# An SSD, MoE and routed-MoE kernel: weights loaded in halves, eight zero products taken out, another written order

## The chip, the cores and the metric

The kernel runs on one core of one Trainium2 chip. The metric is the time of one execution on the device in microseconds (us), of which the trace shows the span from the first to the last instruction. TensorE (matrix products) is PE in the rows and its weight loads are PEld, VectorE is DVE, ScalarE is ACT, GpSimd is POOL. SyncE is SP and issues most of the DMA transfers.

## What is computed

Three stages follow each other: a chunked state-space attention (4 batches, 8 heads, 768 positions), an MoE layer that is one dense block over 3072 tokens, and a routed layer with 8 experts of which each token uses one. Shapes are in the comments.

```python
# attention, per 32-chunk: x (4,8,768,32), a (4,8,768), B and C (4,8,768,16)
cum = np.cumsum(la, axis=-1)                       # la = log(clip(a))
L = np.exp(cum[:, :, :, None] - cum[:, :, None, :]) * causal
y_intra = einsum('bhij,bhjd->bhid', einsum('bhin,bhjn->bhij', Cc, Bc) * L, xc)
y_inter = einsum('bhin,bhnd->bhid', Cc, state) * np.exp(cum)[:, :, :, None]
y[:, :, sl] = y_intra + y_inter                    # and the state is carried on
# dense layer: w_in (256,2048) and w_out (2048,256), float64
h = x @ w_in
x = np.maximum(0.01 * h, h) @ w_out
# routed layer: E=8 experts, w1 (8,256,1024), w2 (8,1024,256)
logits = x @ w_gate + modality_bias[modality_id]
e = argmax(logits); gate = softmax(logits)[e]
out = gate * (np.maximum(x @ w1[e], 0.0) @ w2[e])
```

## The kernel before

**Tiles.** The attention works in chunks of 128 positions, 24 in all (6 a batch). Four chunks make a block of 512 tokens, and the dense layer runs over blocks: for each of 16 slices f of the hidden layer, `h_mm` makes h with six products of 512 columns (two halves of w_in, each as high part times high, high times low, low times high), and `mm2` adds y with six more. The routed layer runs tiles of 512 gathered tokens of one expert with the same three-part products (`e_m1`, `e_m2`), and scatters its rows to the output with indirect DMAs from POOL (`e_sc`).

**Between h and y** stand four steps: `sa` on ACT scales h, `gg` on DVE takes the maximum, `gh` on ACT rounds it to the high part, `gl` on DVE takes what is left. h has two buffers.

**Weights of the dense layer.** w_in and w_out are float64 and are read as 64-bit integers into a tile `raw` (three buffers), a megabyte a piece: four pieces of w_in (`raw.i.k`), four of w_out (`raw.o.k`). Each piece is converted in two parts of 128x512 (`hb`, `lb` on ACT, `or` as two instructions on DVE, `cast` on ACT, and `subv` on DVE or `subg` on POOL for the low part). `part_win(k, kk)` is half kk of piece k, `part_wout(k, q)` the same for w_out. ACT's `cast` writes wih or woh, the last subtraction wil or wol.

**The start.** `decay_a` takes the logarithm of a, transposes it and makes the running sum `cum` with a product of a triangle. For chunks 0 to 3 the exponents come from products into PSUM (`bc`, `exp`). Chunk 0 needs only the logarithms. Chunks 1 to 3 need `cumb`, three bfloat16 parts of the sum: `rows` transposes cum on PE, `high` copies the first part on ACT, `out` writes the rows out (`cumrow`), `cr` on DVE takes the rest, `lows` on ACT casts it, `lowv` on DVE (L387, tile `cumb`) subtracts the third part. After `lowv` come `bc.1`, `exp.1` and so on. Later chunks load their exponents from DRAM (`cumd`, `e`).

**A chunk.** `trmm`, `trc` (tile `cm`), `trb` (tile `btt`), `trd` transpose C and B; `cb` makes their products, `mul` (tile `e`, three instructions) applies the exponents, `p3` makes the output and the state's step, `xa` on ACT and `xb` on DVE write the high and low part (`xh`, `xl`) of the block's input, `st` (tiles `pm`, `st`) carries the state. The first product of the dense layer, h.0 (L694), needs xa.3 and xb.3, the last chunk of block 0.

**Order.** Nothing is reordered by a scheduler: the string `PLAN` lists the steps, `name.chunk.part`, and each engine gets its instructions in this order. SP's DMA issues stand in it too; each has one of eight completion semaphores and waits for the DMA that had it before. Zero products (`zer`) run on PE at some places: six at the very start, two and three in `decay_a` (L346, L347 and L355), five in `warm.1.5` (L1165), four in `wy.4.1` (L1171).

Of the kernel before, what the change touches and what calls it, by code (L numbers as in the profile page):

```python
# [31 lines left out]
    trmm.3 mul.2.1 lx.3 p3.1 mul.2.0 trb.3 hb.o.0.1 trc.3 load.5 mul.2.2 bc.3.0 xa.1 lb.o.0.0 st.1 trd.3 trde.3 xb.1
    or.o.0.0 exp.3.1 p3.2 exp.3.0 bs.3 cb.3 cast.o.0.0 cd.4 st.2 trmm.4 xa.2 mul.3.1 subg.o.0.0 wy.4.1 lb.o.0.1
    mul.3.0 trc.4 le.5 xb.2 trb.4 mask.4 mul.3.2 load.6 trd.4 trde.4 hb.i.1.0 p3.3 or.o.0.1 exp.4.0 xa.3 cd.5 trmm.5
    exp.4.1 xb.3 le.6 st.3 h.0 lx.4 lb.i.1.0 trc.5 raw.o.1 bs.4 mask.5 trb.5 cast.o.0.1 load.7 trd.5 h.1 sa.0 or.i.1.0
    trde.5 exp.5.0 cb.4 subv.o.0.1 sa.1 cast.i.1.0 gg.0 mask.6 hb.i.1.1 mul.4.2 h.2 lb.i.1.1 mul.4.0 subg.i.1.0
    mul.4.1 gh.0 gg.1 trmm.6 exp.5.1 p3.4 or.i.1.1 le.7 h.3 lx.5 xa.4 gl.0 gh.1 lx.6 sa.2 st.4 y.0 trb.6 cast.i.1.1
    trc.6 xb.4 hb.o.1.0 gl.1 sa.3 cb.5 bs.5 load.8 subv.i.1.1 exp.6.0 y.1 gg.2 mask.7 mul.5.0 gh.2 mul.5.1 load.9 h.4
    mul.5.2 lb.o.1.0 gl.2 exp.6.1 gg.3 p3.5 raw.i.2 or.o.1.0 gh.3 le.8 y.2 xa.5 le.9 sa.4 bs.6 lx.7 exp.7.0 cd.7 xb.5
    h.5 load.10 gl.3 gg.4 cb.6 sa.5 cast.o.1.0 y.3 mul.6.0 hb.o.1.1 gg.5 subg.o.1.0 gh.4 mul.6.1 trmm.7 mul.6.2  # L40
    lb.o.1.1 h.6 gh.5 gl.4 trb.7 or.o.1.1 exp.7.1 p3.6 sa.6 trc.7 h.7 bs.7 le.10 xa.6 gg.6 cast.o.1.1 raw.o.2 st.6
    xb.6 raw.i.3 trd.7 y.4 trde.7 gl.5 hb.i.2.0 subv.o.1.1 cb.7 gh.6 mask.9 hb.i.2.1 y.5 mul.7.2 sa.7 mul.7.0 lb.i.2.1
    mul.7.1 trmm.8 gl.6 lb.i.2.0 p3.7 gg.7 y.6 xa.7 gh.7 xb.7 exp.9.1 or.i.2.1 h.16 exp.9.0 gl.7 h.17 or.i.2.0 sa.16
    y.7 gg.16 sa.17 raw.o.3 cast.i.2.0 bs.9 load.11 gg.17 cast.i.2.1 subg.i.2.0 h.18 pV.0 trb.8 gh.16 gh.17 gl.16 h.19
    pA.0 gl.17 hb.o.2.0 trc.8 sa.18 y.16 cd.8 lb.o.2.0 gg.18 lx.8 subv.i.2.1 trd.8 gh.18 y.17 le.11 sa.19 lx.9 gl.18
    gg.19 h.20 or.o.2.0 y.18 sa.20 gh.19 cast.o.2.0 gl.19 h.21 hb.o.2.1 gg.20 subg.o.2.0 y.19 sa.21 mask.8 gh.20 gg.21
    lb.o.2.1 h.22 gl.20 gh.21 or.o.2.1 hb.i.3.0 y.20 lb.i.3.0 sa.22 gl.21 exp.8.0 h.23 or.i.3.0 gg.22 mask.11 y.21
    sa.23 cast.o.2.1 gg.23 gh.22 h.8 cast.i.3.0 gl.22 gh.23 subv.o.2.1 h.9 sa.8 subg.i.3.0 hb.i.3.1 gg.8 lb.i.3.1 y.22
    cd.9 gl.23 sa.9 or.i.3.1 h.10 gh.8 exp.8.1 gg.9 y.23 gl.8 sa.10 cast.i.3.1 h.11 pA.1 pV.1 gh.9 subv.i.3.1 gg.10
    y.8 hb.o.3.1 bs.8 st.7 h.12 gl.9 gh.10 trde.8 sa.11 gl.10 hb.o.3.0 y.9 kg2 gg.11 sa.12 lb.o.3.0 gg.12 mask.10 h.13  # L50
    gh.11 or.o.3.0 y.10 sa.13 gl.11 cast.o.3.0 h.14 kg3 gg.13 exp.10.0 kv2 y.11 gh.12 subg.o.3.0 sa.14 lb.o.3.1 cb.8
    gh.13 gl.12 kd h.15 mul.8.0 gg.14 gl.13 y.12 sa.15 exp.11.1 gg.15 lx.10 h.24 or.o.3.1 gh.14 lx.11 y.13 mul.8.2
    cast.o.3.1 mul.8.1 sa.24 subv.o.3.1 h.25 gh.15 gl.14 cd.10 gg.24 p3.8 sa.25 load.12 gl.15 gg.25 y.14 le.12 y.15
    lx.12 gh.24 gl.24 h.26 evA.0 gh.25 evV.0 bt sa.26 lg.0 exp.10.1 h.27 lt.0 gl.25 trmm.9 sa.27 bs.10 l2.0 load.13
    trc.9 y.24 r1.0 trb.9 xa.8 r2.0 trd.9 trde.9 st.8 exp.11.0 rp.0 yr.0.0 xb.8 y.25 be.0 yc.0.0 gg.26 cb.9 gh.26 h.28
    mul.9.1 mul.9.0 mul.9.2 trmm.10 cd.11 p3.9 trc.10 gg.27 trb.10 rx.0 trd.10 le.13 st.9 trde.10 gh.27 load.14 yr.0.1
    mask.12 xa.9 h.29 yc.0.1 xb.9 sa.28 gl.26 cb.10 gl.27 y.26 mul.10.0 mul.10.1 mul.10.2 trmm.11 gg.28 p3.10 trb.11
    trc.11 gh.28 bs.11 trd.11 load.15 xa.10 h.30 cd.13 exp.12.0 xb.10 st.10 lx.13 y.27 sa.29 gl.28 trde.11 le.14 sa.30
    gg.29 lx.14 cb.11 gh.29 exp.12.1 h.31 mul.11.1 gl.29 mul.11.0 y.28 mul.11.2 cd.14 gg.30 trmm.12 p3.11 y.29 mask.13
    le.15 xa.11 trb.12 gh.30 xb.11 trc.12 sa.31 h.32 gg.31 bs.12 gh.31 gl.30 cb.12 load.16 sa.32 h.33 exp.13.1  # L60
# [1228 lines left out]
```

## Time and profile before

| | |
|---|---|
| time, median of 3 runs | 509.98 us (508.88 to 510.38) |
| time of the profiled execution | 507.78 us |
| its span, first to last instruction | 506.0 us |
| mean granted clock of TensorE | 0.996 |
| busy: PE, DVE, ACT, POOL | 491.9, 324.3, 284.9, 130.4 us |
| HBM read and written | 41.14 and 6.60 MB |

The profiled execution is 2.2 us below the median, and 1.78 us of it lie around the span. Products overlap and their ends are modelled, so PE's share says little; how far a product starts after the one before it says more. A row of a timeline gives start, length, engine, line, operation and tiles, and in brackets how long the engine was idle before it and what ended that.

### The profile page before, as it was taken

The numbers are of one execution on the slowest core, as the hardware profiler recorded it, in microseconds if no ns is written. First come the engines' busy times: TensorE is split into PE (matmuls) and PEld (weight loads), VectorE is DVE, ScalarE is ACT, GpSimd is POOL, SyncE is SP. The second block draws the span as 40 slices with busy tenths as digits, with TensorE's granted clock in tenths as the row PEclk, the third lists the DMA queues.
The fourth block names the chain that finished last, engine by engine and source line by source line (L and its number), as shares of the span: only waits on it lengthen the run. The fifth ranks groups of instructions, "written<-read, shape, count | busy, mean of one in ns | idle before, by whom it ended". The sixth has DMA issues, their size and how long they took to land.

```text
span 506.0 us, 8845 instructions
## 1 busy us (share of the span) xinstructions
PE 491.9 (97%) x3250; PEld 392.2 (78%) x3252; DVE 324.3 (64%) x702; ACT 284.9 (56%) x627; POOL 130.4 (26%) x131
## 2 busy tenths in 40 slices
...
GB/s 196 200 214 230 249 157 2 1 88 22 122 54 107 1 101 130 47 25 135 78 1 2 47 258 44 0 29 120 23 40 149 251 147 218 35 169 2 0 59 74
DMA packets 102454, 48.40 MB, mean 96 GB/s; under 512 B 84065, under 2 KB 93698, under 8 KB 102402
## 3 DMA queue, kind: packets, MB, share of 16 engines
...
q0 software_dynamic: 3072, 6.41, 4.1%
...
HBM read 41.14 MB, written 6.60 MB: 94 GB/s over the span
## 4 chain that ended last, share of the span: by engine, by line
PE 63%; issue 17%; POOL 7%; DVE 4%; DMA 4%; ACT 4%; POOLq 1%; SPq 0%; ACTq 0%
PE y L736 25%; PE h L694 25%; POOL out_dram L1131 4%; PE cb L549 2%; PE psy L591 2%; POOL w2s L1044 2%; DMA il<-ids,pi 2%; POOL xg L1022 1%; PE psy L586 1%; DMA xt<-in_x_dram 1%; PE hp L1070 1%; ACT e L460 1%; DVE gl L716 1%; PE yr L897 1%; PE lp L779 1%
## 5 line engine op out<-in xcount | busy, mean ns | idle before, releaser
L701 ACT ACTIVATE sa<-h 128x512 f32<-128x512 f32 x96 | 57.5, 598 | 58.8 <-PE h L694 58.6
L706 DVE TENSOR_TENSOR gg<-sa,h 128x512 f32<-128x512 f32 x96 | 65.2, 681 | 26.2 <-ACT sa L701 25.6
L694 PE MATMUL h<-xh,wih 128*128 128x512 f32 x192 | 79.1, 412 | 1.7 <-ACT xh L609 0.9
L716 DVE TENSOR_TENSOR gl<-gg,gh 128x512 fp32r<-128x512 f32 x96 | 67.1, 702 | 19.8 <-ACT gh L711 18.4
L736 PE MATMUL y<-gh,woh 128*128 128x512 f32 x192 | 79.2, 412 | 0.0
L736 PE MATMUL y<-gl,woh 128*128 128x512 f32 x192 | 75.3, 392 | 0.2
L694 PE MATMUL h<-xl,wih 128*128 128x512 f32 x192 | 75.2, 392 | 0.0
L736 PE MATMUL y<-gh,wol 128*128 128x512 f32 x192 | 75.1, 391 | 0.0
L694 PE MATMUL h<-xh,wil 128*128 128x512 f32 x192 | 75.0, 391 | 0.0
L711 ACT CAST gh<-gg 128x512 fp32r<-128x512 f32 x96 | 59.1, 619 | 21.5 <-DVE gg L706 18.2
L1088 DVE SCALAR_TENSOR_TENSOR hl<-hp,hh 128x512 fp32r<-128x512 f32 x48 | 33.1, 690 | 58.4 <-ACT hh L1084 58.4
L1101 PE MATMUL o<-w2s,hh 128*128 128x256 f32 x384 | 70.3, 282 | 0.0
L1070 PE MATMUL hp<-x2h,w1s 128*128 128x512 f32 x192 | 67.3, 396 | 0.1
L1101 PEld LDWEIGHTS o<-w2s,hh 128*128 128x128 f32 x384 | 61.8, 190 | 3.1
L1084 ACT ACTIVATE hh<-hp 128x512 fp32r<-128x512 f32 x48 | 28.6, 599 | 61.3 <-PE hp L1070 51.8
L1101 PE MATMUL o<-w2s,hl 128*128 128x256 f32 x192 | 54.1, 282 | 0.0
L460 ACT ACTIVATE e<-e,ncum 128x128 f32<-128x128 f32 x160 | 50.8, 397 | 0.0
L442 POOL TENSOR_SCALAR_AFFINE_SELECT e<-e 128x1024 f32<-128x1024 f32 x20 | 22.9, 1150 | 102.4 <-DMA e<-cumd 78.0
L694 PEld LDWEIGHTS h<-xh,wih 128*128 128x128 f32 x192 | 36.2, 188 | 15.5 <-issue 3.6
L880 POOL DMA_INDIRECT il<-ids,pi x24 | 25.9, 1077 | 81.6 <-DVE base L871 59.0
L736 PEld LDWEIGHTS y<-gh,woh 128*128 128x128 f32 x192 | 36.1, 188 | 10.6 <-issue 3.3
L694 PEld LDWEIGHTS h<-xh,wil 128*128 128x128 f32 x192 | 36.0, 188 | 7.9
...
## 6 DMA issues: line engine op xcount, KB each, us to landing
...
```

Source lines behind the costliest of these rows:

```text
L460: s.activation(out=e[:, h, :], in_=i, func=AF.Exp, bias=ncum[:, cc, b * H + h:b * H + h + 1])
L694: t_.matmul(h, lhsT=w[:, k, fs], rhs=xx[:, k, :], start=(i == 0), stop=(i == 5))
L701: s.activation(out=d["sa"], in_=d["h"], func=AF.Copy, scale=0.01)
L706: v.tensor_tensor(out=d["gg"], in0=d["sa"], in1=d["h"], op=ALU.max)
L711: s.copy(out=d["gh"], in_=d["gg"])
L716: v.tensor_tensor(out=gl, in0=d["gg"], in1=d["gh"].bitcast(F32), op=ALU.subtract)
L736: t_.matmul(y_t[j][k], lhsT=w[:, f, ds], rhs=gg, start=(f in first and i == 0), stop=(f in last and i == 2))
L880: w = g.indirect_dma_start(out=il[:], out_offset=IndirectOffsetOnAxis(ap=pi[:, q:q + 1], axis=0), in_=ids[:, c0 + q:c0 + q + 1], in_offset ...
L1070: t_.matmul(d["hp", f], lhsT=d[1][:, k, part, fs], rhs=xx[:, k, :], start=(n == 0), stop=(n == 5))
L1084: s.activation(out=e_h(i, f, "hh"), in_=ex[i]["hp", f], func=AF.Relu)
L1088: v.scalar_tensor_tensor(out=e_h(i, f, "hl"), in0=d["hp", f], scalar=0.0, in1=d["hh", f].bitcast(F32), op0=ALU.max, op1=ALU.subtract)
L1101: t_.matmul(d["o", q], lhsT=d[h, f][:, q * P:(q + 1) * P], rhs=d[2][:, f, part, :], start=(start and n == 0), stop=(f == NF2 - 1 and n == ...
```

## The change

Three things change. `load_win` and `load_wout` move half a piece (512 KB) instead of a whole one, so there are 16 weight transfers instead of 8, and `PLAN` has `raw.i.0.0` ahead of the first loads of C and B. Eight zero products go: the three at the end of `decay_a` and the five of `warm.1.5`. `PLAN` is another order from its first to its last line; of it two lines stand here for each side.

```diff
--- before.py
+++ after.py
@@ -24,100 +24,101 @@
 PLAN = """
-    load.0 raw.i.0 kg1 load.1 decay_a kvb bc.0.1 kvc decay_b bc.0.0 exp.0.1 load.2 trmm.0 hb.i.0.0 rows trc.0 trb.0
-    raw.o.0 exp.0.0 lx.0 cb.0 load.3 end high cd.1 bs.0 out warm.1.5 cr mul.0.0 hb.i.0.1 mul.0.2 trmm.1 lows trd.1
 ...
+    raw.i.0.0 load.0 kg1 raw.i.0.1 lx.0 decay_a load.1 hb.i.0.0 bc.0.1 lb.i.0.0 decay_b kvc or.i.0.0 bc.0.0 exp.0.1
+    trmm.0 exp.0.0 load.2 rows trc.0 bs.0 cast.i.0.0 kvb load.3 trb.0 high subg.i.0.0 end cb.0 out cr mul.0.1
 ...
@@ -351,8 +352,6 @@
         t_.matmul(p1[:, 0:NCB * BH], lhsT=tri, rhs=laT.rearrange("p c r -> p (c r)"), start=True, stop=True)
         cum = ap_.tile([P, NCB, BH], F32, tag="cum", name="cum", bufs=1)
         v.tensor_copy(cum.rearrange("p c r -> p (c r)"), p1[:, 0:NCB * BH])
-        for _ in range(3):
-            t_.matmul(p0[:, 256:512], lhsT=zer[:, 0:P], rhs=zer[:, 0:256], start=True, stop=True)
         dk["cum"] = cum
 
     def decay_b():
@@ -651,10 +650,10 @@
     raws = {}
     NPC = DFF // 512
 
-    def load_win(k):
-        r = rawp.tile([P, 2, 512], w_in.dtype, tag="raw", name="raw")
-        nc.sync.dma_start(out=r, in_=w_in[:, k * 512:(k + 1) * 512].rearrange("(k p) f -> p k f", p=P))
-        raws["i", k] = r
+    def load_win(k, kk):
+        if kk == 0:
+            raws["i", k] = rawp.tile([P, 2, 512], w_in.dtype, tag="raw", name="raw")
+        nc.sync.dma_start(out=raws["i", k][:, kk, :], in_=w_in[kk * P:(kk + 1) * P, k * 512:(k + 1) * 512])
 
     def part_win(k, kk):
         os = slice(k * 512, (k + 1) * 512)
@@ -667,10 +666,11 @@
             woh[:, os, :].rearrange("p a d -> p (a d)"), wol[:, os, :].rearrange("p a d -> p (a d)"),
         )
 
-    def load_wout(k):
-        r = rawp.tile([P, 4, DM], w_out.dtype, tag="raw", name="raw")
-        nc.sync.dma_start(out=r, in_=w_out[k * 512:(k + 1) * 512, :].rearrange("(k p) f -> p k f", p=P))
-        raws["o", k] = r
+    def load_wout(k, q):
+        if q == 0:
+            raws["o", k] = rawp.tile([P, 4, DM], w_out.dtype, tag="raw", name="raw")
+        o = k * 512 + 2 * q * P
+        nc.sync.dma_start(out=raws["o", k][:, 2 * q:2 * q + 2, :], in_=w_out[o:o + 2 * P, :].rearrange("(k p) f -> p k f", p=P))
 
     xt_t, g_t, y_t = {}, {}, {}
 
@@ -1200,7 +1200,7 @@
         "load": attn_load, "lx": attn_load_x, "le": attn_load_e, "cumd": decay_store, "pA": part_a, "pV": part_v, "kg1": consts_g1, "kvb": consts_vb,
         "kvc": consts_vc, "kg2": consts_g2, "kv2": consts_v2, "kg3": consts_g3, "kd": consts_dma, "cd": attn_cd, "mask": attn_mask, "exp": exp, "bc": bc_mm, "trmm": tr_mm, "trc": tr_c, "trb": tr_b, "trd": tr_d,
         "trde": tr_de, "cb": cb_mm, "bs": cb_bs, "mul": cb_mul, "p3": p3_mm, "xa": p3_xa, "xb": p3_xb, "st": p3_st,
-        "raw": lambda t, k: (load_win if t == "i" else load_wout)(k),
+        "raw": lambda t, k, q: (load_win if t == "i" else load_wout)(k, q),
         "h": lambda f: h_mm(f // NF, f % NF), "sa": lambda f: h_sa(f // NF, f % NF), "gg": lambda f: h_gg(f // NF, f % NF),
         "gh": lambda f: h_gh(f // NF, f % NF), "gl": lambda f: h_gl(f // NF, f % NF), "y": lambda f: mm2(f // NF, f % NF),
         "evA": evict_a, "evV": evict_v, "lg": logits_mm, "lt": logits_lt, "l2": logits_l2, "r1": route_1, "rx": route_x, "r2": route_2,
```

**The program's start on SP and ACT.** SP's first issues, ahead the transfer of a; ct and bt are C and B of a chunk, xt is x, raw the weights. Before:

```order
L1157 DMA a_sb<-in_a_dram 96x256
L419 DMA ct<-in_C_dram 128x8x16
L420 DMA bt<-in_B_dram 128x8x16
L656 DMA raw<-in_moe_w_in_dram 128x2x512
L419 DMA ct<-in_C_dram 128x8x16
L420 DMA bt<-in_B_dram 128x8x16
```

Now:

```order
L1157 DMA a_sb<-in_a_dram 96x256
L656 DMA raw<-in_moe_w_in_dram 128x512
L418 DMA ct<-in_C_dram 128x8x16
L419 DMA bt<-in_B_dram 128x8x16
L656 DMA raw<-in_moe_w_in_dram 128x512
L427 DMA xt<-in_x_dram 128x8x32
```

The first half of the first weight piece moved ahead of C and B of chunk 0, the second half behind them, and x of chunk 0 came up.

ACT from the table's warm-up (`tab`) to `lows` (L384, L383 now); e<-bc are the exponentials of chunk 0, L376 (L375) is `high`. Before:

```order
L341 ACTIVATE tab<-tab 1x8
L360 ACTIVATE ecum<-cum 128x192
L460 ACTIVATE e<-bc,ncum 128x128 x4
L634 ACTIVATE hb<-raw 128x512
L508 COPY btt<-ps 128x128
L460 ACTIVATE e<-bc,ncum 128x128 x4
L376 CAST cumb<-p_251 96x512
L392 COPY cumrow<-p__264 32x256
L392 COPY cumrow<-p_251 32x512
L634 ACTIVATE hb<-raw 128x512
L384 CAST cumb<-cr 64x512
```

Now:

```order
L342 ACTIVATE tab<-tab 1x8
L633 ACTIVATE hb<-raw 128x512
L638 ACTIVATE lb<-raw 128x512
L359 ACTIVATE ecum<-cum 128x192
L459 ACTIVATE e<-bc,ncum 128x128 x8
L1186 CAST wih<-hb 128x512
L507 COPY btt<-ps 128x128
L375 CAST cumb<-p_255 96x512
L391 COPY cumrow<-p__268 32x256
L391 COPY cumrow<-p_255 32x512
L383 CAST cumb<-cr 64x512
```

`hb.i.0.0` and `lb.i.0.0` moved ahead of `ecum`, the eight exponentials stand together, the first `cast` came ahead of `high`, and `hb.i.0.1` went behind `lows`.

**DVE around `lowv`.** From the step before `cr` (L380, L379 now) on; L387 (L386) is `lowv`, L558 and L561 (L557, L560) are `mul`, L644 with L645 (L643 with L644) is one `or`. Before:

```order
L450 TENSOR_TENSOR cd<-ct,ecum 128x128
L538 TENSOR_TENSOR bs<-bt,e 128x128
L380 TENSOR_TENSOR cr<-p_251,cumb 64x512
L558 TENSOR_TENSOR e<-e,cb 128x256
L561 TENSOR_TENSOR e<-e,cb 128x512
L496 TENSOR_TENSOR cm<-ps,par 128x256
L387 TENSOR_TENSOR cumb<-cr,cumb 32x512
L644 SCALAR_TENSOR_TENSOR hb<-hb,lb 128x512
L645 SCALAR_TENSOR_TENSOR hb<-raw,hb 128x512
L644 SCALAR_TENSOR_TENSOR hb<-hb,lb 128x512
```

Now:

```order
L399 COPY cend<-p_255 32x4
L379 TENSOR_TENSOR cr<-p_255,cumb 64x512
L557 TENSOR_TENSOR e<-e,cb 128x256
L449 TENSOR_TENSOR cd<-ct,ecum 128x128
L557 TENSOR_TENSOR e<-e,cb 128x256
L386 TENSOR_TENSOR cumb<-cr,cumb 32x512
L560 TENSOR_TENSOR e<-e,cb 128x512
L449 TENSOR_TENSOR cd<-ct,ecum 128x128
L643 SCALAR_TENSOR_TENSOR hb<-hb,lb 128x512
L644 SCALAR_TENSOR_TENSOR hb<-raw,hb 128x512
```

Between `cr` and `lowv` stand two short `mul` and a `cd` instead of a short and a long `mul` and a `cm`. Earlier on DVE, around the first `cm` (L496, L495 now; L359 is `ncum`), stood:

```order
L272 TENSOR_REDUCE par<-mask_104 128x2
L273 TENSOR_TENSOR gm<-mask_104 128x128
L359 TENSOR_SCALAR ncum<-cum 128x192
L496 TENSOR_TENSOR cm<-ps,par 128x256
L400 COPY cend<-p__264 32x2
```

and stands now:

```order
L274 TENSOR_TENSOR gm<-mask_104 128x128
L643 SCALAR_TENSOR_TENSOR hb<-hb,lb 128x512
L644 SCALAR_TENSOR_TENSOR hb<-raw,hb 128x512
L495 TENSOR_TENSOR cm<-ps,par 128x256
L537 TENSOR_TENSOR bs<-bt,e 128x128
```

The first `or` (hb<-hb,lb and hb<-raw,hb) moved ahead of the first `cm`.

**PE between the routing's two products of block 0.** l (L793) is the transposed logits, rp (L849) the ranks, which need DVE's one-hot `ohb`; y (L736) and h (L694) are the dense layer's. Before:

```order
L793 MATMUL l_1635<-ident,lt 128x128
L736 MATMUL y<-gh,woh 128x512
L736 MATMUL y<-gl,woh 128x512
L736 MATMUL y<-gh,wol 128x512
L736 MATMUL y<-gh,woh 128x512
L736 MATMUL y<-gl,woh 128x512
L736 MATMUL y<-gh,wol 128x512
L514 MATMUL ps<-ident,cd 128x128
L849 LDWEIGHTS tris
```

Now:

```order
L793 MATMUL l_1612<-ident,lt 128x128
L694 MATMUL h<-xh,wih 128x512
L694 MATMUL h<-xl,wih 128x512
L694 MATMUL h<-xh,wil 128x512
L694 MATMUL h<-xh,wih 128x512
L694 MATMUL h<-xl,wih 128x512
L694 MATMUL h<-xh,wil 128x512
L513 MATMUL ps<-ident,cd 128x128
L736 MATMUL y<-gh,woh 128x512
L736 MATMUL y<-gl,woh 128x512
L736 MATMUL y<-gh,wol 128x512
L736 MATMUL y<-gh,woh 128x512
```

Six products of h came in between, and y moved behind the transpose of cd.

## Rows read from the trace of the kernel before

**Rows 1.** Busy us of each engine in two stretches, clock, DMA share.

```profile
13.00:31.00 18.00, 15.40 (x187) 9.67 (x188) 17.06 (x42) 14.64 (x37) 3.73 (x3) 1.00 0.92 183
31.00:500.00 469.00, 465.52 (x2990) 375.83 (x2990) 302.70 (x642) 261.98 (x572) 122.53 (x110) 1.00 0.39 90
```

**Rows 2.** Who PE waited for from 31 us on: total, times, longest.

```profile
PE h L694 <- ACT xh L609: 0.9, 1, 0.9
PE h L694 <- DVE gg L706: 0.9, 3, 0.4
PE rp L849 <- DVE ohb L827: 0.6, 1, 0.6
PE yr L897 <- ACT cdt L529: 0.4, 1, 0.4
```

**Rows 3.** PE in order of time, from the start to h.0.

```profile
1.27 2.74 PE L1153 MATMUL wps<-zer 128*128 128x512 bf16 x6 [1.27 <-DVE tab L1150]
...
5.64 0.85 PE L355 MATMUL p<-zer 128*128 128x256 bf16 x3
6.29 0.63 PE L468 MATMUL bc<-mk,id 128*128 128x512 bf16 x1
...
11.48 1.03 PE L1165 MATMUL bc<-zer 128*128 128x512 bf16 x4 [0.16 <-issue]
13.44 0.33 PE L490 MATMUL ps<-ident,ct 128*128 128x128 f32 x1 [0.93 <-DVE e L558]
...
31.23 0.50 PE L694 MATMUL h<-xh,wih 128*128 128x512 f32 x1 [0.88 <-ACT xh L609]
```

**Rows 4.** ACT in order of time, up to xa.3.

```profile
4.87 0.21 ACT L341 ACTIVATE tab<-tab 1x8 f32<-1x8 f32 x1
...
8.07 1.14 ACT L460 ACTIVATE e<-bc,ncum 128x128 f32<-128x128 f32 x4 [1.42 <-PE bc L477]
9.09 0.69 ACT L634 ACTIVATE hb<-raw 128x512 f32<-128x512 f32 x1
...
30.82 0.36 ACT L609 CAST xh<-psy 128x256 fp32r<-128x256 f32 x1
```

**Rows 5.** DVE in order of time, up to xb.3.

```profile
9.39 0.42 DVE L496 TENSOR_TENSOR cm<-ps,par 128x256 f32<-128x256 f32 x1 [2.20 <-PE ps L491]
...
12.38 0.68 DVE L380 TENSOR_TENSOR cr<-p,cumb 64x512 f32<-64x512 f32 x1 [0.89 <-ACT cumrow L392]
12.98 0.40 DVE L558 TENSOR_TENSOR e<-e,cb 128x256 f32<-128x256 f32 x1
13.31 0.67 DVE L561 TENSOR_TENSOR e<-e,cb 128x512 f32<-128x512 f32 x1
...
14.48 0.68 DVE L387 TENSOR_TENSOR cumb<-cr,cumb 32x512 bf16<-32x512 f32 x1
...
31.21 0.42 DVE L615 TENSOR_TENSOR xl<-psy,xh 128x256 fp32r<-128x256 f32 x1 [0.42 <-ACT xh L609]
```

**Rows 6.** DVE's groups, 15.17 to 31.2 us: busy us, mean ns, idle before.

```profile
L644 DVE SCALAR_TENSOR_TENSOR hb<-hb,lb 128x512 int32<-128x512 int32 x4 | 2.9, 737 | 0.0
L645 DVE SCALAR_TENSOR_TENSOR hb<-raw,hb 128x512 int32<-128x512 int32 x4 | 2.8, 692 | 0.1
...
L496 DVE TENSOR_TENSOR cm<-ps,par 128x256 f32<-128x256 f32 x3 | 1.3, 418 | 0.0
...
L450 DVE TENSOR_TENSOR cd<-ct,ecum 128x128 f32<-128x128 f32 x4 | 1.1, 285 | 0.0
...
L1188 DVE TENSOR_TENSOR wil<-hb,wih 128x512 fp32r<-128x512 f32 x1 | 0.7, 685 | 0.0
```

**Rows 7.** The first weight piece's DMA: issue at 2.4 us, time to landing.

```profile
L656 SPq DMA_DIRECT2D raw<-in_moe_w_in_dram x1: 582/582/582, 2.4 to 2.4; - x1
...
DMA to landing us min/median/max: 5.5/5.5/5.5
```

**Rows 8.** POOL's last scatter.

```profile
499.60 0.97 POOL L1131 DMA_INDIRECT out_dram<-o,gi  x1 [0.60 <-ACT o L1127]
```

More of the change, by code (lines that the diff above doesn't have):

```diff
@@ L32 @@
[L32 to L60, printed above, removed]
-    mul.12.1 mul.12.0 mul.12.2 trmm.13 gg.32 y.30 trb.13 r3.0 gl.31 h.34 gh.32 sa.33 gg.33 y.31 sa.34 trc.13 h.35
@@ new lines @@
+    trmm.0 exp.0.0 load.2 rows trc.0 bs.0 cast.i.0.0 kvb load.3 trb.0 high subg.i.0.0 end cb.0 out cr mul.0.1
+    raw.o.0.0 lows fullmm cd.1 mul.0.0 cumd hb.i.0.1 lowv raw.o.0.1 trmm.1 trd.1 lb.i.0.1 mul.0.2 lx.1 bc.1.0 trde.1
+    cd.2 lx.2 or.i.0.1 bc.1.1 full trb.1 p3.0 exp.1.1 trc.1 cast.i.0.1 cd.3 trmm.2 exp.1.0 st.0 bc.2.1 subv.i.0.1 xa.0
+    hb.o.0.0 trc.2 cb.1 bs.1 trb.2 xb.0 exp.2.1 trd.2 mul.1.1 bc.2.0 lb.o.0.0 load.4 mul.1.0 mul.1.2 trde.2 bc.3.1
+    exp.2.0 or.o.0.0 trmm.3 hb.o.0.1 cb.2 le.4 exp.3.1 p3.1 raw.i.1.0 bs.2 cast.o.0.0 trc.3 lx.3 mul.2.0 lb.o.0.1
```

151 lines of the change are left out of this document (89 added, 62 removed).

## The prediction

> **What bounds the kernel now.** I read the busy times in two stretches first. From 31 us to 500 us PE is busy 465.52 of 469.00 us [rows 1], and the list of its waits in the same stretch names 2.8 us in all (0.9, 0.9, 0.6 and 0.4) [rows 2]. So from the first product of the dense layer, h.0 at 31.23 us, PE alone sets the pace, and a reordering of ACT, DVE or POOL can win at most those 2.8 us there. Ahead of h.0 it is different. From 13 to 31 us DVE is busy 17.06 of 18.00 us while PE has room (15.40) and ACT too (14.64) [rows 1]. DVE's last work there, xb.3 at 31.21, follows xa.3 on ACT at 30.82, and h.0 waits for xa.3 [rows 3 to 5]. So the start is bound by a chain up to `lowv` (14.48 us) and then by DVE's list of work. What the change is worth is decided by when h.0 can start, since the work of PE behind it is the same: the zero products removed all lie ahead of it.
>
> **The change, part by part.** I count from the profiled execution (507.78 us, of which 506.0 us are the span).
>
> Three zero products (end of `decay_a`). They run from 5.64 to 6.29 us at 0.22 us each, which is 256 columns at TensorE's lower level of 1.2 GHz, directly ahead of the first product of `bc.0.1` [rows 3]. ACT waits 1.42 us for that step before its first exponentials at 8.07 us [rows 4]. So they lie on the path, and their removal moves it by 0.65 us if the products behind keep their speed. TensorE goes over to 2.4 GHz between 6.29 us and 11.48 us (six zero products of 512 columns took 2.74 us at the start, four take 1.03 us later [rows 3]). If it does so at the same moment and not behind the same product, more of `bc.0.1` runs at the lower level and half of the gain is lost. Ends 0.3 and 0.65; I take 0.5, as only the products up to the change of level suffer.
>
> The five zero products of `warm.1.5` run from 11.48 us, and the next product waits for DVE until 13.44 us [rows 3]. They delay nothing; removing them is worth 0 as long as TensorE keeps its level (below).
>
> The first weight half and its conversion. `hb.i.0.0` and `lb.i.0.0` now stand ahead of `ecum` and the exponentials on ACT. They take 0.69 us each (`hb` in rows 4; `lb` has the same 128x512). ACT is free at 5.08 us, and the first exponentials come at 8.07 less 0.5 = 7.57 us. With 0.4 us for `ecum` (an estimate: an exponential of 128 columns takes 1.14/4 [rows 4], this one has 192), 0.7 us are to spare: `hb` may start up to 5.8 us. The half piece is issued at about 1.3 us, behind the load of a alone. The whole piece took 5.5 us behind two small loads [rows 7]; half the bytes take between half of that and all of it, so it lands between 4.1 and 6.8 us, and nearer 5 us with nothing but a in front. So nothing waits in the likely case, and the cost is 0. Behind `hb` on ACT wait `ecum`, both exponentials of chunk 0, `btt` and `high`; if it came at 6.8 us they would all be 1.0 us late. On DVE the `or` (0.74 + 0.69 us [rows 6]) moves into the idle 2.20 us ahead of the first `cm` [rows 5]; it costs 0 there, where it had cost 1.43 us in the saturated list.
>
> From `cr` to `lowv`. Before: 12.38 to 14.48, 2.10 us, as `lowv` stood behind a short and a long `mul` and a `cm` [rows 5]. Now the list is `cr` (0.60 to the next start), a short `mul` (0.33 to the next), `cd` (0.285 [rows 6]) and a short `mul` (0.33): 1.55 us. `lows` on ACT, a cast of 64x512, has those 0.95 us behind `cr` to finish. Gain 0.55 us; at the ends 0.3 (if `lows` comes late) and 0.6.
>
> DVE's list from `lowv` to xb.3. Against before, one `or` is gone (-1.43), a `cm` came in that had run ahead (+0.42), a second subtraction of a weight part runs on DVE ahead of h.0 (+0.69) [rows 6], and a long `mul` stands there where a short one stood (0.67 - 0.40 = +0.27 [rows 5]). Sum -0.05 us: the list is as long as before, but has done 0.69 us more of later work. Of the 0.94 us that DVE idles from 13 to 31 us [rows 1], 0.42 us stood directly before xb.3, because xa.3 came late on ACT [rows 5], where four exponentials of chunk 4 were queued ahead of it. Now those stand behind xa.3. I take 0.4 us; the ends are 0 and 0.94.
>
> So h.0 comes 0.5 + 0.55 + 0.05 + 0.4 = 1.5 us earlier, near 29.7 us. PE's work behind it is unchanged.
>
> The waits behind h.0. The two named waits in the routing of block 0 are 0.6 us (rp for DVE's one-hot) and 0.4 us (yr for ACT) [rows 2]. Six more products of h now stand between the logits and rp, so the first is covered; yr.0.1 stands one `p3` further from the transpose whose copy it waited for. That is 1.0 us off, and the reordered rest will bring waits of its own at other places; I take 0.4 us as the balance. Ends: 2.8 us gained if no wait is left, and 1.5 us lost.
>
> The other seven pieces in halves, eight DMAs more. None of PE's waits behind 31 us is for a DMA [rows 2], so they cost 0 while the order keeps its lead.
>
> The end. The last scatter starts at 499.60 us, 0.60 us idle before it for the last `o` on ACT [rows 8], which is behind PE's last products. That order is the same in both, so the end moves with PE: 0.
>
> **Sum:** 1.5 + 0.4 = 1.9 us, 505.9 us where the profiled execution took 507.78. The median of the runs is 509.98, so I forecast 508.1 us. By the ends alone it would lie between 504.9 (0.65 + 0.6 + 0.05 + 0.94 + 2.8 us off the median) and 510.8 (0.3 + 0.3 + 0.05 gained, 1.5 lost).
>
> **The rivals.**
>
> *The reordered rest eats the lead.* PE is at its limit for 469 us, and each y has to find its gl ready. All steps behind h.0 are in another order, and one missed distance costs some 0.4 us (the longest wait for gg [rows 2]). Four or five such misses cost 1.9 us: no change, 509.9 us. For it: ACT and DVE are nearly full at first, 17.06 of 18 us. Against it: before, only six such waits were left in 469 us, and the distances of h, y and their steps are of the same kind in both orders.
>
> *TensorE stays longer at, or falls back to, 1.2 GHz.* This one ends slower. The place is PE between 11 and 31 us: without the five zero products the stretch from 11.48 to 13.44 us holds less work. In it the level did not fall, with 0.93 us of idle time in front of the transpose [rows 3]; what up to 2.0 us would do, no row shows. PE is busy 15.40 of 18 us behind it [rows 1], so at half the rate each us there loses up to 0.43 us. 8 us at the lower level lose 3.4 us, which is the point from which the kernel is slower by over 0.3%; the whole stretch to 31 us loses 7.7 us less the gain, 515.8 us. A few us before 13 us cost what was gained, 509.7. The Trainium skill (TensorE: Matmul & The Clock Gate, "Why this matters for your kernels") tells to leave no long idle spells between bursts of products, because TensorE falls back to half rate after one. By that rule the zero products earn their place and this rival is the forecast; by the row of the idle time that was survived, the sum above stands.
>
> *The loads come late.* From 13 to 31 us the DMA engines are busy 0.92 of the time [rows 1], each half is one more transfer, and C, B and x of the first chunks now queue behind or between halves. If `hb` starts at 6.8 us, or a transfer of chunks 1 to 3 comes a us late, the lead is 0.5 us or less: 509.5 us. Against it: the same bytes are moved, and the first C and B were there early.
>
> **How the numbers follow.** From no change a difference of 0.3% (1.5 us) is about what a measurement of this kernel can tell. The forecast, lead kept, gets 0.6; its own range is 506.3 to 509.0, and as its middle lies little over the line, 0.48 of it is faster and 0.12 the same. The rest eating the lead 0.2 (0.15 same, 0.05 slower), TensorE's level 0.1 (0.03 same, 0.07 slower), late loads 0.1 (0.08 same, 0.02 slower). In sum 0.48 faster, 0.38 same, 0.14 slower. For 8 in 10 the range reaches from 505.5 (most of the waits gone) to 510.8 (the first and third rival held, most of the second left out).
>
> **What would show it.** Right: the first exponentials on ACT near 7.6 us with `hb` and `lb` ahead of them and no wait for the raw tile worth more than some 0.7 us; `lowv` near 13.4 us; h.0 near 29.7 us; PE's waits behind h.0 of about 2.4 us with none for rp of block 0; the last scatter some 1.9 us earlier. Wrong: a wait of ACT for raw past 5.8 us, steps of products at 1.2 GHz behind 13 us, or waits of PE behind h.0 of over 4 us.

## The result, and the profile after

The changed kernel is slower: 513.44 us (median of 8 runs, 512.52 to 515.93) against 509.55 us of the kernel before in the same batch (8 runs, 508.11 to 512.36; a batch is a set of runs measured together), a ratio of 1.0085, 95% interval 1.0056 to 1.0114. The forecast was 508.1 us, in a range of 505.5 to 510.8. The profiled execution took 515.31 us, of which 513.6 are the span.

First the start: PE of the changed kernel in order of time, and one row from far behind.

```profile
11.55 1.02 PE L404 MATMUL pd<-cend,bsel 32*128 32x6 f32 x8 [0.99 <-ACT cumrow L391]
13.56 0.33 PE L489 MATMUL ps<-ident,ct 128*128 128x128 f32 x1 [0.99 <-DVE e L557]
...
14.27 0.61 PE L469 MATMUL bc<-negm,cumb 96*128 96x512 bf16 x1
...
29.74 0.67 PE L577 MATMUL psy<-cdt,st 128*128 128x256 f32 x2 [2.05 <-DVE st L626]
...
32.12 0.78 PE L694 MATMUL h<-xh,wih 128*128 128x512 f32 x1
...
412.77 0.50 PE L1070 MATMUL hp<-x2h,w1s 128*128 128x512 f32 x1 [2.53 <-DVE hl L1088]
```

h.0 comes at 32.12 us, 0.89 us later than before [rows 3], not 1.5 earlier. Two idle spells of 0.99 us in the place where the five zero products used to run, and one of 2.05 us, stand ahead of it, and the product of 512 columns at 14.27 takes 0.61 us. In the kernel before the same product took 0.39 us:

```profile
15.22 0.39 PE L470 MATMUL bc<-negm,cumb 96*128 96x512 bf16 x1
```

The windows of the changed kernel tell why. Each line gives a stretch and its length, the busy us of PE, PEld, DVE, ACT and POOL, the granted clock as a share of 2.4 GHz, the DMA share and GB/s.

```profile
13.00:31.00 18.00, 15.34 (x176) 9.18 (x177) 16.79 (x40) 14.38 (x36) 2.38 (x2) 0.91 0.97 220
31.00:500.00 469.00, 463.19 (x2963) 374.63 (x2956) 300.81 (x641) 261.15 (x569) 120.18 (x106) 0.99 0.41 89
10.00:14.00 4.00, 2.02 (x20) 1.50 (x20) 3.13 (x8) 2.41 (x6) 0.97 (x1) 1.00 0.99 101
14.00:18.00 4.00, 4.00 (x39) 2.48 (x38) 3.03 (x8) 2.52 (x8) 0.00 (x0) 0.57 1.08 311
...
31.00:35.00 4.00, 3.58 (x18) 2.80 (x11) 3.34 (x7) 2.45 (x9) 1.09 (x1) 0.57 0.83 179
...
405.00:420.00 15.00, 12.47 (x69) 10.99 (x69) 3.69 (x6) 6.38 (x10) 6.42 (x5) 0.89 0.51 171
```

Before, the clock was 1.00 from 13 to 500 us [rows 1]. Now TensorE is granted 1.2 GHz from 14.26 to 17.68, from 31.33 to 34.74 and from 413.62 to 417.03 us (the trace's clock records), each time behind a spell in which it did little: 2.02 us busy of the 4 us from 10 to 14, and the idle spells of 2.05 and 2.53 us in the rows above.

ACT of the changed kernel in order of time:

```profile
5.58 0.67 ACT L633 ACTIVATE hb<-raw 128x512 f32<-128x512 f32 x1 [0.56 <-DMA raw<-in_moe_w_in_dram]
...
6.96 2.16 ACT L459 ACTIVATE e<-bc,ncum 128x128 f32<-128x128 f32 x8
```

And its DVE:

```profile
9.80 1.20 DVE L270 TENSOR_SCALAR negm<-id 96x8 bf16<-96x8 bf16 x1
...
11.96 0.68 DVE L379 TENSOR_TENSOR cr<-p,cumb 64x512 f32<-64x512 f32 x1 [0.84 <-ACT cumrow L391]
...
13.53 0.68 DVE L386 TENSOR_TENSOR cumb<-cr,cumb 32x512 bf16<-32x512 f32 x1
...
31.59 0.42 DVE L614 TENSOR_TENSOR xl<-psy,xh 128x256 fp32r<-128x256 f32 x1 [0.66 <-ACT xh L608]
```

The exponentials begin at 6.96 us (8.07 before [rows 4]) and `hb` is there in time. But `cr` is only 0.4 us earlier than before [rows 5], since `negm`, an operation on 96x8 elements, takes 1.20 us, and `cend`, `cumrow` and `cr` stand behind it. POOL at that time, and its last scatter:

```profile
9.71 1.27 POOL L1188 TENSOR_TENSOR wil<-hb,wih 128x512 fp32r<-128x512 f32 x1 [5.18 <-ACT wih L1186]
...
506.04 0.98 POOL L1131 DMA_INDIRECT out_dram<-o,gi  x1 [0.30 <-issue]
```

`negm` ends at 11.00, 0.02 us behind POOL's subtraction of the first weight half. And from the last scatter's start to the end are 7.6 us, where it had been 6.4 (499.60 [rows 8] to 506.0). Last, whom PE waited for from 31 us on (in us: total, times, longest), 5.6 us in all against 2.8 before [rows 2]:

```profile
PE hp L1070 <- DVE hl L1088: 2.5, 1, 2.5
PE y L736 <- DVE gl L716: 0.8, 2, 0.5
PE h L694 <- DVE gg L706: 0.5, 1, 0.5
PE rp L849 <- DVE ohb L827: 0.5, 1, 0.5
PE psy L590 <- DVE e L557: 0.5, 1, 0.5
PE ps L489 <- ACT cdt L528: 0.4, 1, 0.4
PE cb L548 <- ACT cdt L528: 0.4, 1, 0.4
```

So there are four suspects: TensorE's level in the start, `negm` beside POOL, the 1.2 us behind the last scatter, and the wait of 2.5 us near 410 us.

### The profile page after: what moved, and what is told of

Its sections match the earlier page's. It is cut to its first block, busy times and chain, and to the rows that moved or that the text cites. A ratio compares the mean times of both kernels' runs of the same rounds, so it can differ in the third digit from the quotient of the medians.

```text
span 513.6 us, 8862 instructions
## 1 busy us (share of the span) xinstructions
PE 492.4 (96%) x3243; PEld 394.4 (77%) x3244; DVE 324.7 (63%) x702; ACT 285.5 (56%) x627; POOL 131.6 (26%) x131
## 4 chain that ended last, share of the span: by engine, by line
PE 83%; issue 7%; DVE 4%; POOL 2%; ACT 2%; DMA 1%; POOLq 0%; SPq 0%; ACTq 0%
PE h L694 26%; PE y L736 25%; PE hp L1070 10%; PE o L1101 9%; PE cb L548 3%; PE psy L590 2%; POOL out_dram L1131 2%; PE psy L585 1%; PE yr L897 1%; PE lp L779 1%; PE xps L1051 1%; DMA raw<-in_moe_w_in_dram 1%; PE ps L489 1%; DVE gl L716 1%; PE ps L513 0%
## 5 line engine op out<-in xcount | busy, mean ns | idle before, releaser
L694 PE MATMUL h<-xh,wih 128*128 128x512 f32 x192 | 79.6, 415 | 0.5 <-DVE gg L706 0.5
L716 DVE TENSOR_TENSOR gl<-gg,gh 128x512 fp32r<-128x512 f32 x96 | 69.4, 726 | 16.6 <-ACT gh L711 15.3
L736 PE MATMUL y<-gh,woh 128*128 128x512 f32 x192 | 78.7, 410 | 0.0
L736 PE MATMUL y<-gl,woh 128*128 128x512 f32 x192 | 75.3, 392 | 0.8 <-DVE gl L716 0.8
L694 PE MATMUL h<-xl,wih 128*128 128x512 f32 x192 | 75.6, 394 | 0.0
L694 PE MATMUL h<-xh,wil 128*128 128x512 f32 x192 | 75.5, 393 | 0.0
L736 PE MATMUL y<-gh,wol 128*128 128x512 f32 x192 | 75.1, 391 | 0.0
L694 PEld LDWEIGHTS h<-xh,wih 128*128 128x128 f32 x192 | 36.6, 191 | 13.0 <-issue 4.2
L736 PEld LDWEIGHTS y<-gh,woh 128*128 128x128 f32 x192 | 36.0, 188 | 10.7 <-issue 2.3
L1070 PEld LDWEIGHTS hp<-x2h,w1s 128*128 128x128 f32 x192 | 36.3, 189 | 10.3 <-DVE hl L1088 3.4
L880 POOL DMA_INDIRECT il<-ids,pi x24 | 24.6, 1025 | 71.2 <-DVE base L871 58.4
```

The costliest lines, as they stand in the source:

```text
L694: t_.matmul(h, lhsT=w[:, k, fs], rhs=xx[:, k, :], start=(i == 0), stop=(i == 5))
L716: v.tensor_tensor(out=gl, in0=d["gg"], in1=d["gh"].bitcast(F32), op=ALU.subtract)
L736: t_.matmul(y_t[j][k], lhsT=w[:, f, ds], rhs=gg, start=(f in first and i == 0), stop=(f in last and i == 2))
L880: w = g.indirect_dma_start(out=il[:], out_offset=IndirectOffsetOnAxis(ap=pi[:, q:q + 1], axis=0), in_=ids[:, c0 + q:c0 + q + 1], in_offset ...
L1070: t_.matmul(d["hp", f], lhsT=d[1][:, k, part, fs], rhs=xx[:, k, :], start=(n == 0), stop=(n == 5))
```

## The experiments

All ratios are to the kernel before, run in the same batch. Its medians were 506.95 us in the first batch (first four runs below), 507.03 in the second, 509.81 in the third and 507.15 in the last, so runs are compared within a batch where they can be. Each run has 10 executions, e3 has 4 and e4 has 8. "h.0" is the start of h.0 in us, "2.4 from" the time at which the level first rose, "level" the stretches at 1.2 GHz between that and the last products, all three of the one profiled execution. The theories that are tested have letters; each is told in the expectation in which its letter first stands.

```
run                ratio   95% interval      h.0    2.4 from  level at 1.2 GHz
e1_zeros_back      1.0027  1.0009 to 1.0044  32.71  7.16      31.05-34.46
e2_gaps_filled     1.0010  0.9999 to 1.0022  31.12  4.10      none
e3_start_only      1.0080  1.0050 to 1.0109  33.41  6.90      13.73-20.55
e4_before_no_zeros 1.0031  1.0013 to 1.0050  32.70  5.91      12.74-19.57
e5_before_halves   1.0001  0.9988 to 1.0014  31.02  4.12      14.36-17.77
e6_second_gap      1.0022  1.0009 to 1.0035  33.48  6.49      13.32-20.14
e7_negm_early      0.9989  0.9974 to 1.0004  29.73  4.06      none
e8_gaps_whole      1.0010  0.9988 to 1.0033  32.49  6.97      none
e9_best            0.9995  0.9974 to 1.0016  29.94  5.48      none
e10_before_shift   1.0021  0.9995 to 1.0048  31.25  7.28      none
e11_after_shift    1.0046  1.0030 to 1.0062  32.76  5.99      12.82-19.65, 412.18-415.59
e12_start_fixed    0.9997  0.9976 to 1.0018  31.28  6.82      none
e13_after_again    1.0034  1.0019 to 1.0049  32.20  5.17      12.00-18.82
e14_gaps_again     1.0008  0.9991 to 1.0025  31.48  6.37      none
e15_best_again     0.9970  0.9956 to 0.9984  29.83  3.92      none
e16_old_experts    0.9996  0.9979 to 1.0013  30.35  4.39      none
```

**The level.** e1 puts the eight zero products back into the changed kernel:

```diff
+        for _ in range(3):
+            t_.matmul(p0[:, 256:512], lhsT=zer[:, 0:P], rhs=zer[:, 0:256], start=True, stop=True)
-    ... out cr ...
+    ... out warm.1.5 cr ...
```

> The changed kernel with the eight zero products put back: three of 256 columns at the end of decay_a, five of 512 behind `out`. Theory A (the level): the changed kernel is slower because TensorE falls to 1.2 GHz at 14.3 and again at 31.3 us, each time behind idle time that the zero products would have filled or followed; each fall costs about 1.7 us. The five behind `out` lie ahead of the first fall, so that one goes: about 511.7 us, the granted clock of the run near 0.989 in place of 0.986, products of bc.1.0 at full rate; the fall at 31.3 stays, as its idle time (27.7 to 29.7) has the same zero products in front as before. Theory B (the rest): the start is as good as forecast and what is lost is lost behind 60 us, in waits that the new order of the rest brings (4.9 us in the stretch from 400 to 420 alone); then this run is 513.4 us or up to 0.5 slower, for the three on the path.

e2 fills the three idle spells instead:

```diff
-    ... out cr ...    ... lowv raw.o.0.1 trmm.1 ...          ... wy.4.1 ...
+    ... out warm.1.5 cr ...    ... lowv raw.o.0.1 warm.1.4 trmm.1 ...    ... wy.12.1 ...
```

> The changed kernel with zero products of 512 columns in the three idle spells of TensorE that I see in the start: five behind `out`, four ahead of the transposes of chunk 1, and twelve in place of four ahead of the p3 of chunk 3; none in decay_a. Theory A: no fall before 40 us, so 3.4 us less than the changed kernel, about 510.0 us, granted clock 0.992 or above, h.0 near 30.4 us. Theory B: 512.9 to 513.4 us, the waits behind 60 us as they were, whatever the level does in the start.

e3 joins the start of the changed kernel (up to h.0) to the rest of the one before; e4 is the kernel before without its eight zero products.

> The changed kernel's order up to and with h.0, then what is left in the order of the kernel before (halves side by side). No zero products but the four of wy. Theory A: the falls at 14 and 31 us stay, 512 to 513 us. Theory B: the waits and the third fall between 400 and 420 us go (4.9 us of excess there against 0.9 before), the time is 508.5 to 509.5 us. If both hold in part, about 510.5 us: two falls paid for with 3.4 us, a start that is 1.5 us earlier, no loss behind it.

> The kernel before with its eight zero products left out and nothing else. Theory A: TensorE is then idle from 11.3 to 13.4 us and falls to 1.2 GHz behind it for some 3.4 us; 1.0 to 1.7 us slower than before, 510.5 to 511.2 us, granted clock 0.992 to 0.993 where it was 0.996. Theory B, and the reading of my prediction: no fall; 0.3 to 0.6 us faster for the three on the path, 509.0 us.

e4 loses 0.31% by nothing but the zero products, and e2 keeps the level: theory A. The profiles of all runs side by side say it more firmly. The six that leave the first gap unfilled (the changed kernel, e3, e4, e6, e11, e13) all fell between 12.0 and 14.3 us, whether the level had risen at 4.02 or at 6.90 us; of the twelve that fill it only e5 fell there. e3 is slow without the new rest, as theory A has it; but 1.1 us of its loss is a wait for btt at the seam of the two orders, so it weighs less. Here is e4 from 14 to 18 us:

```profile
14.00:18.00 4.00, 4.00 (x20) 2.81 (x21) 3.34 (x6) 1.99 (x6) 0.00 (x0) 0.50 0.76 113
```

And e2 from 10 to 14 and from 14 to 18 us:

```profile
10.00:14.00 4.00, 3.84 (x28) 2.27 (x29) 3.13 (x8) 2.42 (x6) 1.03 (x1) 1.00 1.01 110
14.00:18.00 4.00, 3.38 (x50) 2.08 (x47) 3.93 (x10) 3.26 (x10) 0.00 (x0) 1.00 1.05 310
```

e1 keeps the first fall away but not the second, as expected. e6 fills the last gap alone:

```diff
-    ... wy.4.1 ...
+    ... wy.12.1 ...
```

> The changed kernel with twelve zero products in place of four ahead of the p3 of chunk 3 (26.9 us) and nothing else. Theory A, each fall of the level priced alone: the fall at 14 us stays, that at 31 us goes; 1.7 us less than the changed kernel, ratio to before 1.005. If the first fall carries nearly all of the loss (it delays DVE's list, the second only h.0), the ratio is 1.007 to 1.0085; if the falls are not the cause, 1.0085.

Its ratio of 1.0022 was expected at 1.005, counted from a changed kernel at 1.0085; e13 will show that this figure was that batch's. Beside e13 (1.0034) neither e6 nor e1 (1.0027) mends more than the intervals are wide: in both the level still falls once. And e11 and e13, which leave the last gap unfilled, did not fall behind it, as the changed kernel and e1 did at 31 us: that this gap has to be filled is not shown.

**The halves.** e5 loads the kernel before's pieces as two halves side by side (raw.i.1 becomes raw.i.1.0 raw.i.1.1, and so on); e8 is e2 with whole loads at the place of the first halves.

> The kernel before with every weight piece loaded as two halves, one directly behind the other, all else (order, zero products) as before. My prediction's step and theory A: no change, ratio 0.999 to 1.001, no fall of the clock ahead of the last stretch, h.0 near 31.2 us. If eight more transfers hurt (late loads), h.0 comes 0.5 to 1.0 us later and the ratio is 1.001 to 1.002.

> The run with the three gaps filled, but with each weight piece loaded whole at the place where its first half stood (the first ahead of all other loads). If the halves matter: the first piece lands 5 to 6 us behind its issue, hb.i.0.0 starts near 7 us in place of 5.6 with the exponentials queued behind it, h.0 is 0.5 to 1.0 us later, ratio 1.002 to 1.003. If they don't: h.0 near 31.1 us and ratio 1.001.

e5 is at 1.0001, 0.9988 to 1.0014: eight more transfers cost nothing that these runs can tell. e8 has the same ratio as e2; its `hb` came at 6.85 us and h.0 at 32.49, but its level also rose 2.9 us later, so the gain of the half load alone can't be told.

**negm.** e7 is e2 with kvb moved:

```diff
-    ... bs.0 cast.i.0.0 kvb load.3 ...      ... decay_b kvc or.i.0.0 ...
+    ... bs.0 cast.i.0.0 load.3 ...          ... decay_b kvb kvc or.i.0.0 ...
```

> The run with the three gaps filled, and the step kvb (three short operations on DVE, negm the last) put ahead of kvc, so that DVE does them at 6.2 us and not at 9.4. Theory C: with the level held the lead is lost because negm takes 1.20 us in place of 0.17 while POOL subtracts the first weight half (9.76 to 11.03 us), and cend, cumrow and cr stand behind it. Then cend comes at 10.0 us, cr near 11.1 (12.01 with the gaps filled), lowv near 12.6, h.0 near 30.2, and the ratio to before is 0.999 (1.0010 with the gaps filled). Theory D: the lead is lost in DVE's saturated list and at xa.3 and trmm.5 ahead of h.0, whatever comes before; then cr is earlier and h.0 still near 31.1 us, ratio 1.001.

DVE of e7 in order of time:

```profile
6.40 0.17 DVE L270 TENSOR_SCALAR negm<-id 96x8 bf16<-96x8 bf16 x1
...
10.84 0.68 DVE L379 TENSOR_TENSOR cr<-p,cumb 64x512 f32<-64x512 f32 x1 [0.64 <-ACT cumrow L391]
```

And its first product of the dense layer on PE:

```profile
29.73 0.48 PE L694 MATMUL h<-xh,wih 128*128 128x512 f32 x1
```

`negm` takes 0.17 us again, `cr` comes 1.2 us earlier than in e2 (12.01), h.0 1.4 us: theory C in size and place. The ratio falls by 0.0021, 1.1 us; e2 and e7 ran in two batches, and by the two intervals it is anything from 0.1 to 2.0 us. By the Trainium skill (SBUF — State Buffer, "SBUF: two separate sides") VectorE in some of its modes and GpSimd take one pair of ports by turns, each for a whole instruction. The end of `negm` 0.02 us behind POOL's subtraction agrees; that it was the port, no run here shows.

**The end.** h.0 is now 1.5 us ahead of before and TensorE's last product ends 2.4 us earlier (496.37 to 498.81; 1.5 us earlier than in e5, which has the old order and ran in e7's batch), but e7 is only 0.6 us faster: 8.2 us lie between its last scatter and the end. No view prints POOL's waits there; the trace's records have them. POOL runs through a branch and then five waits (start of each in us; in front the number of POOL's records, the padding drains of e9 to e11 and e15 included):

```
before            305   502.68  502.79  502.85  502.94  503.02
changed           311   508.44  508.55  510.90  510.99  511.07
e7_negm_early     311   500.32  500.43  502.62  502.70  502.79
e10_before_shift  311   504.21  504.32  506.46  506.55  506.63
e12_start_fixed   306   505.98  506.09  506.15  506.24  506.41
e15_best_again    319   500.40  500.51  500.57  500.66  500.75
e16_old_experts   312   500.58  502.94  503.01  503.10  503.19
```

All kernels with the changed rest and no padding have a hole of 2.2 to 2.4 us behind the second wait; in the changed one two instruction transfers begin around it (508.46 and 509.10). The kernel before has two such transfers in the same place (502.89 and 503.30) and no hole, so the transfers alone don't bring it. Two theories, and padding to tell them apart: e9 is e7 with eight drains on POOL, e10 the kernel before with six, e11 the changed kernel with eight.

```diff
-    ... kg1 ...
+    ... kg1 dr dr dr dr dr dr dr dr ...
```

> The run with negm early, and eight drains on POOL behind its constants, where it is idle; they compute nothing and only move POOL's later instructions on by eight places. Theory F (code): in all runs with the changed kernel's rest POOL stands still for 2.2 us between the second and the third of its last waits, while an instruction transfer is under way; the place of that hole goes with the number of instructions ahead of it. Then the hole goes, the stretch from TensorE's last product to the end is 6.7 us in place of 8.9, and the ratio to before is 0.9946 (0.9989 with the hole). Rival G (scatters): POOL waits there for the scatters, which the new order brings later; then the hole stays and the ratio is 0.999.

> The kernel before and six such drains on POOL, by which its last waits stand at the same place of the instruction stream as in the changed kernel. Theory F: a hole of 2.2 us comes up behind the second of POOL's last waits, the stretch behind TensorE's last product is 8.8 us in place of 7.2, and the ratio to before is 1.003. Rival G: 1.000, no hole.

> The changed kernel and eight drains on POOL, nothing else. Theory F: the 2.2 us behind TensorE's last product go and nothing else changes: ratio to before 1.004 (1.0085 without the drains), granted clock near 0.986. Rival G: 1.0085.

The hole comes in e10, goes in e9 and e11, and stands one wait earlier in e16, which has 312 records and not 311: it goes with the place in POOL's instruction stream, as theory F says, and not with the scatters. What it costs in time is less sure: e10 is 1.1 us slower than before, but its interval reaches from nothing to 0.5%, and where the hole goes POOL may wait for the last scatter instead (1.0 us in e9 and e11). By the Trainium skill (Runtime: NRT & Kernel Launch, "Instruction fetch mechanics") a taken branch to code that isn't loaded stalls until it is fetched; the 2.6 us from branch to first wait in the kernel before (500.09 to 502.68) agree. That the second hole is the same kind of thing one stretch of code later is argued, not shown. e9 missed its 0.9946: it has the wait near 410 us, which e7 had not.

**The rest.** e12 has e7's order up to h.0, then that of the kernel before.

> The order of the run with negm early (gaps filled with zero products) up to and with h.0, and behind it the order of the kernel before. It has the lead at h.0 (29.7 us, 1.5 us ahead of before) with the rest of before and no hole at the end. If the new order of the rest costs nothing of its own, this is as fast as the run with negm early and the drains, 0.995 to 0.997. If the new rest gains by its fewer waits, this one is slower than that by up to 0.002; if the new rest eats the lead, this one is the faster, and the other stays at 0.997 or above.

It is undecided: h.0 came at 31.28 us in its profile, where the level rose late (6.82), and at the seam PE waits 1.8 us for btt of ACT at 34.7 us, which neither order has.

**In one batch.** The last batch repeats the changed kernel, e2 and e9 unchanged, and e16, which is e9 with all behind y.95 in the order of before.

> The changed kernel once more, on the chip of the next three. 1.0085 to before, as first measured, if the loss does not depend on the chip. If the wait of 2.5 us near 410 us (with the fall of the level behind it, 1.7 us) belongs to a slower chip, the ratio is 1.004 to 1.005 on a chip where it is missing.

> The run with the three gaps filled, again. Theory A (level): 3.4 us less than the changed kernel beside it, a difference of the two ratios of 0.006 to 0.007. If most of the difference between the two first calls was the wait near 410 us, it is 0.003 or less.

> The run with gaps filled, negm early and the eight drains, again. By the sum of the parts (negm 1.0 us, POOL's hole 2.2 less 1.0 for the last scatter that is then waited for) 2.2 us less than the run with the gaps filled: 0.0043 below its ratio. If the lead is lost again in the rest, 0.002 or less below it.

> The run before this one, with what is left behind y.95 (the experts' part, from 358 us) in the order of the kernel before. If the wait of 2.5 us for hl belongs to the new order of the experts' part: it is missing here on any chip, and where the run before this one has it, this one is 2.5 us faster or more. If it belongs to the chip alone: it is here as well, or in neither, and the two are the same within 0.001.

The changed kernel is at 1.0034 here, and the wait near 410 us is missing in all four. Filling the gaps takes off 0.0026 (1.3 us, interval 0.7 to 2.0), the smaller of the two sizes expected; the mean granted clock of its ten executions is 0.995 to 0.996, against 0.987 to 0.993 in e13, so the fall is not the profiled execution's alone. `negm` and the drains take off 0.0038 (1.9 us; 2.2 were expected). e16 differs from e15 in the hole and in the order of the experts; their last products end together (496.65 and 496.64) and it is 1.3 us slower. e15 is faster than both kernels, by 0.3% (0.16 to 0.44%) than before. Its waits of PE from 29 us on:

```profile
PE ps L489 <- DVE e L557: 0.8, 1, 0.8
PE h L694 <- DVE gg L706: 0.5, 2, 0.3
PE psy L590 <- DVE e L557: 0.5, 1, 0.5
PE ps L489 <- ACT cdt L528: 0.4, 1, 0.4
PE rp L849 <- DVE ohb L827: 0.4, 1, 0.4
PE cb L548 <- ACT cdt L528: 0.4, 1, 0.4
```

The first of these waits, at 36.41 us, takes back most of the lead at h.0. From e14 to e15 h.0 comes 1.65 us earlier (31.48 to 29.83), PE's transpose behind that wait only 0.95 us (37.36 to 36.41), the next product of h 0.5 us, and the last product of all none (496.47 to 496.64). In e15 the `or` behind h.0 falls beside POOL's mask and subtraction, and takes 1.29 and 1.67 us. DVE and POOL of e15:

```profile
33.02 1.29 DVE L643 SCALAR_TENSOR_TENSOR hb<-hb,lb 128x512 int32<-128x512 int32 x1
34.35 1.67 DVE L644 SCALAR_TENSOR_TENSOR hb<-raw,hb 128x512 int32<-128x512 int32 x1
35.95 0.41 DVE L557 TENSOR_TENSOR e<-e,cb 128x256 f32<-128x256 f32 x1
```

```profile
32.68 1.09 POOL L441 TENSOR_SCALAR_AFFINE_SELECT e<-e 128x1024 f32<-128x1024 f32 x1 [6.58 <-DMA e<-cumd]
33.85 1.62 POOL L1188 TENSOR_TENSOR wil<-hb,wih 128x512 fp32r<-128x512 f32 x1
```

In e14 the same two operations lie between POOL's and take 0.68 and 0.69 us:

```profile
34.99 0.68 DVE L643 SCALAR_TENSOR_TENSOR hb<-hb,lb 128x512 int32<-128x512 int32 x1
35.71 0.69 DVE L644 SCALAR_TENSOR_TENSOR hb<-raw,hb 128x512 int32<-128x512 int32 x1
```

So in this pair of profiles all that e15 is ahead lies behind the last product (6.6 us to the end against 8.9), and what `negm` alone is worth in the time is not shown beyond e2 to e7. No run moved this `or`.

e9, the same kernel in the batch where before took 509.81 us, had one row more:

```profile
PE hp L1070 <- DVE hl L1088: 2.5, 1, 2.5
```

That wait is in three profiled runs, the changed kernel's first, e9 and e11, all in the batches in which before took 509.6 to 509.8 us and all with the new order of the rest; e10 and e12 in such a batch, with the old one, don't have it. In it ACT waits for a product that PE's records show as done 2.5 us earlier (408.89, seen by ACT at 411.38). Whether something of those batches (the chip, say), the order of the experts' part or both bring it stays open, as the last batch had no such wait to mend.

## Why the prediction was wrong

Three steps that I priced at nothing cost more than the sum gained, and one term, the waits behind h.0, had the wrong sign. With the three mended, e15 is 1.5 us faster than before where 1.9 were forecast. That it comes so near is partly luck: some of it is a stretch behind the last product that the padding makes shorter than the kernel before's (6.6 us against 7.2), which no term of the sum had.

**"Removing them is worth 0 as long as TensorE keeps its level."** It did not. This was the second rival, given 0.1, and the place was right. By the rule of the Trainium skill that I cited there it was the forecast; the level did fall, but the rule speaks of long idle spells, and here no single one from 10 to 14 us was over 0.99 us. The row on which I relied, 0.93 us survived, had 2.91 us of work around it in 10 to 14 us; the changed kernel has 2.02. (These four microseconds are not all: e5 had 3.07 in them and fell.) The rival's own price was off: I charged PE's lost work (0.43 us for each us), which would make 2.9 us of 6.8, but PE has room in the start, and 6.8 us at the lower level cost 1.3 us of the time (e13 to e14; 1.6 for the kernel before, e4, where the three products on the path go as well).

**The first weight half, "the cost is 0".** `hb` was in time (5.58 us; the bound was 5.8), ACT's exponentials began early and the `or` found its idle time, all as said. What I left out of the moved steps is POOL's subtraction, which follows the cast: it now runs at 9.7 us, and kvb's `negm`, moved behind the exponentials, falls under it and takes 1.20 us in place of 0.17. h.0 comes 1.4 us earlier without that, the time falls by 1.1 us (0.1 to 2.0, e2 to e7).

**"The end moves with PE: 0."** The order of the last scatters is indeed the same, but POOL's instructions ahead of them are six more, and code that stands elsewhere stalls: 2.2 us in the profile, 1.1 us of the time by e10, whose interval includes nothing, and 1.3 from e15 to e16, which differ in the experts' order too.

**"Waits behind h.0", -0.4.** From h.0 on PE waited 1.9 us before (the 2.8 us of [rows 2] hold the 0.88 us ahead of h.0 itself, which I so counted in two terms) and waits 2.6 us in e15: 0.7 lost, not 0.4 gained. The first rival held that much. The largest, 0.8 us, is the `or` beside POOL; yr's wait is gone as forecast, rp still waits (0.4 to 0.5), six products more did not cover it.

The other steps. `cr` to `lowv`: 1.57 us, forecast 1.55, right. h.0 near 29.7: 29.73, 29.83, 29.94 and 30.35 in e7, e15, e9 and e16, 31.28 in e12, 32.12 and 32.20 in the changed kernel. So 29.7 was met, but by luck in part, since the way there differs: `lowv` is at 12.4 to 12.7 in the first three and not at 13.4, and the list behind it up to xb.3 takes 16.9 us in e7 where it took 16.7 before [rows 5] and 16.3 were forecast, as xa.3 still comes late (0.80 us idle before xb.3; I had taken 0.4 back). In those three the level rose at 3.92 to 5.48 us; e12, the same kernel up to h.0, where it rose at 6.82, has `lowv` at 13.32 and no lead at h.0 over the kernel before (7.25 us, 31.23). How much of the lead comes with an early rise is not shown. The zero products of `decay_a`: the exponentials were 1.1 us earlier in the profiled run, but the level rose at 4.02 us there and at 7.25 before, so that term can't be read from this pair. The halves: 0, right as far as e5 can tell. The loads came in time.

Of the 1.0085 of the first measurement the last batch shows 1.0034; the difference, 2.6 us, has the size of the wait near 410 us, but that this is its cause in all eight runs is argued, not shown.
